# Moving three pieces of preparation in a two-block kernel: a matrix quarter, a square root, and the row of inverse sums

## The chip, the cores and the metric

The kernel runs on one core of one Trainium2 chip. A core has five engines that run side by side, each through its own list of instructions in order: TensorE (PE in the profile, with its weight loads as PEld), VectorE (DVE), ScalarE (ACT), GpSimd (POOL) and SyncE (SP, which here issues nearly all transfers). They meet at semaphores. The metric is the device time of one execution in microseconds. The kernel before takes 1575.92 us, the median of three runs (1575.31 to 1576.35).

## The reference

Two blocks follow each other. The first is attention with a threshold, over 8 batches of 8 heads, 576 rows and 64 columns:

```python
scores = scale * np.matmul(q, k.transpose(0, 1, 3, 2))
thresh = np.max(scores, axis=-1, keepdims=True) - tau
scores = np.where(scores >= thresh, scores, -1000000000.0)
scores = scores - np.max(scores, axis=-1, keepdims=True)
attn = np.exp(scores)
attn = attn / (np.sum(attn, axis=-1, keepdims=True) + 1e-09)
return np.matmul(attn, v).astype(np.float32)
```

The heads are put side by side into x (8, 576, 512). The second block mixes x by a Fourier transform over rows and columns, normalizes each row, and runs two matrices with a relu between them:

```python
u = x + np.real(np.fft.fft(np.fft.fft(x, axis=1), axis=2))
un = (u - mean(u)) / np.sqrt(var(u) + 1e-06)
out = u + np.maximum(un @ w_ch1, 0.0) @ w_ch2
```

w_ch1 is 512x2048 and w_ch2 2048x512, and both arrive as 64-bit floats. All work on the chip is in 32-bit floats.

## The kernel before

**Steps.** Work goes by pairs of heads, four pairs to a batch, five steps to a pair: four steps of 128 rows of both heads, and one that takes the last 64 rows of both. So a batch is 20 steps; steps are counted through: 0 to 19 are the first batch (`step`, L1509), 20 to 39 the second (`second_batch`, L1661), the rest a third loop (L1743). The order of every engine's list is the order in which this Python code emits instructions (a schedule by hand); the only choice left to a planner is `fill`, which emits matmuls of the second block up to a budget counted in matmul columns.

**One step** in the first two batches. `scores` (L451, L457) multiplies into two PSUM tiles. `softmax` (L463) takes the row maximum on VectorE (neg, L472), the exponential on ScalarE (e, L480) with a small threshold instruction (thr, L484), and the comparison and sum on VectorE (e, L488). `inverse` (L394) turns the sums into den (L396, L399) on VectorE. `transposed_weights` (L568) then turns the weights of the step before on TensorE (pe L598 and L601, pw L616), and ScalarE copies them out of PSUM (ends L604 or L608, e_t L618 or L620). In these two batches the division is made late: `spread_inverse` (L512) copies den over 128 columns into rec (L520) on ScalarE, rec is turned along with the weights of that step one step later (L601), and VectorE multiplies by it after the product with v (x, L656). In a pair's fifth step, `spread_inverse` also copies the end of e (L515). From the third batch on, e is divided at once (L560) and rec isn't needed.

**Converting the matrices.** Each 128x512 piece ("chunk") of the two matrices goes through `convert` (L279): a transfer, two bit operations on VectorE (L296, L299), two ScalarE instructions (L304, L307), one VectorE sum (L311), a GpSimd product (L316), and last a sign on ScalarE (L318) with a second GpSimd product (L319). A chunk takes two steps. `softmax` calls its VectorE parts and L316 between the maximum and the exponential (argument `meanwhile`). Its last stage, L318 and L319, is called by the argument `behind`, after the exponentials and before the inverse. The L304 and L307 of the next chunk follow after the weights' copies, and `spread_inverse` is the last thing of a step. The first matrix's first three quarters (12 chunks) are converted in steps 0 to 12; its last quarter and the second matrix in steps 20 to 39, after `PLAN`, which has two chunks at once in steps 25, 30, 32 and 35.

**Centring.** The mean over the rows of the first matrix is taken off it. For each quarter `column_means` (L371, 4 matmuls of 512 columns into pm) is followed by a ScalarE copy (`copy_mean`, L1591) and one step later by `mirrored` (L381, two matmuls into pr) and four `less_mean` (L387, two on VectorE, two on GpSimd). In the first batch they take the place of `busy` (pd, L111), one or two matmuls whose result nobody reads. Quarters 0, 1 and 2 stand in steps 7 and 8, 10 and 12, 14 and 15. The last quarter is centred in steps 29 and 31.

**Mixing of the first batch** in steps 20 to 22: VectorE folds (L698 to L760), six products py (L770) copied by ScalarE (L775), then pa (L787) and the sums u_t (L812, L816) on GpSimd and VectorE. The first product of the hidden layer, ph (L913), reads u_t. Each block of ph has 4 matmuls and a relu, on ScalarE (L918) for even blocks and VectorE (L920) for odd ones. After every third, `Rows.load` turns 128 rows of u (pn, L862), ScalarE copies them out (L867, L868) and VectorE takes their statistics (L873, L874).

**Square root.** `Rows.factors` (L883) takes the square root of the variances (L885) and then one exponential of a constant (L888). For the first group of rows it is called after block 12, in step 36. For all other groups a list, `wanted`, is looked at in the third loop after the division of e.

**PSUM and queues.** The tiles of pe, pw, pv, pm, pr, pn, py, pa and ph share four banks, given out in turn as they come free. SyncE's queue holds the loads of q, k and v, the two small transfers that swap rows of x (L672, L674), and the chunks' loads (L286), in the order of emission.

Of the kernel before, what the change touches and what calls it, by code (L numbers as in the profile page):

```python
# [47 lines left out]
def kernel(  # L48
# [12 lines left out]
    nc = tc.nc  # L61
# [7 lines left out]
    NJ = HID // 128  # L69
# [390 lines left out]
                )  # L460
        steps[i] = (sc, nh)

    def softmax(i, between=None, meanwhile=None, behind=None):  # L463


        t = i % NT
        sc, nh = steps[i]
        neg = sb.tile([128, 2], FP32, tag="neg", bufs=3, name="neg")
        thr = sb.tile([128, 2], FP32, tag="thr", bufs=3, name="thr")
        e = sb.tile([128, 2 * S], FP32, tag="e", name="e")  # L470
        for j in range(nh):
            nc.vector.tensor_reduce(  # L472
                out=neg[:, j : j + 1], in_=sc[j][:, :, 0:HALF], axis=AXIS_XY, op=ALU.max,
                negate=True,
            )
        if meanwhile is not None:
            meanwhile()
        for j in range(nh):
            ej = e[:, S * j : S * (j + 1)].rearrange("p (c n) -> p c n", c=2)
            nc.scalar.activation(  # L480
                out=ej, in_=sc[j][:, :, 0:HALF], func=ACT.Exp, bias=neg[:, j : j + 1], scale=1.0
            )
            if j == 0:
                nc.scalar.activation(  # L484
                    out=thr[:, 0:nh], in_=neg[:, 0:nh], func=ACT.Identity,
                    bias=thr_off[:, :], scale=-1.0,
                )
            nc.vector.scalar_tensor_tensor(  # L488
                out=ej, in0=sc[j][:, :, 0:HALF], scalar=thr[:, j : j + 1], in1=ej,
                op0=ALU.is_ge, op1=ALU.mult, accum_out=den_eps[i % 3][:, j, 0:1],  # L490
            )
            if between is not None and j == 0:
                next(between)
        if behind is not None:
            behind()
        den = inverse(i, nh)
        if between is not None:
            for _ in between:
                pass
        if normalized(i // NT):  # L500
            nc.vector.tensor_scalar(
                out=e[:, 0:S], in0=e[:, 0:S], scalar1=den[:, 0:1], scalar2=None, op0=ALU.mult
            )
            if nh == 2:
                nc.scalar.activation(
                    out=e[:, S : 2 * S], in_=e[:, S : 2 * S], func=ACT.Copy, scale=den[:, 1:2]
                )
            steps[i] = (e, None)
        else:
            steps[i] = (e, den[:, 0:nh])  # L510
# [57 lines left out]
    def transposed_weights(i):  # L568
        for _ in weights_in_parts(i):
            pass  # L570
# [337 lines left out]
    def channels(rows):  # L908
        for j in range(NJ):
            ht = hs[:, BT * j : BT * (j + 1)]  # L910
            ph = ps.tile([128, 512], FP32, tag="mm", bufs=4, name="ph")
            for c in range(ND):
                nc.tensor.matmul(  # L913
                    ph[:, :], w1[c][:, 128 * j : 128 * (j + 1)], u_t[:, c, 0:BT],
                    start=(c == 0), stop=(c == ND - 1),
                )
            if j % 2 == 0:
                nc.scalar.activation(out=ht, in_=ph[:, :], func=ACT.Relu)  # L918
            else:
                nc.vector.tensor_relu(ht, ph[:, :])  # L920
            yield 4 * ND * BT
            if j % 3 == 2 and j // 3 < 4:
                rows.load(j // 3)
                yield ND * 128
            if j == 12:
                rows.factors()
        def both():
            yield from w1_forms()
            ensure(1)
            while not next(forms_w2):  # L930
                yield

        forms = both()
        for t in range(4):
            po = ps.tile([128, DM], FP32, tag="mm", bufs=4, name="po")
            for j in range(NJ):
                nc.tensor.matmul(  # L937
                    po[:, :], hs[:, BT * j + 128 * t : BT * j + 128 * (t + 1)], w2[j],
                    start=(j == 0), stop=(j == NJ - 1),
                )  # L940
                if j % 2 == 1 and j < NJ - 1:
                    next(forms, None)
                    yield 2 * 4 * DM
            rows.add(t, slice(0, DM), po[:, :])
            rows.store(t)
            background()
            yield 2 * 4 * DM
        for _ in forms:
            pass
# [499 lines left out]
    wanted = []  # L1449
# [59 lines left out]
    def step(i):  # L1509

        n, t = divmod(i, NT)
        scores(i)

        def stages(count):
            for _ in range(count if i - 1 in chunks else 0):
                next(chunks[i - 1], None)

        def next_stages():
            if i in chunks:
                next(chunks[i])  # L1520
            stages(2)

        def last_stage():
            stages(1)
            chunks.pop(i - 1, None)

        if t == 1 and n > 0:
            softmax(i, values_in_parts(n - 1, 1), next_stages, last_stage)
            load_v(n + 1)
        elif t == 3:  # L1530
            softmax(i, values_in_parts(n, 0), next_stages, last_stage)
        else:
            softmax(i, None, next_stages, last_stage)
        if t == 1 and n > 0:
            pass
        elif later and later[0][0] <= i:
            later.pop(0)[1](i)
        else:
            busy(2 if i < NCHUNK else 1)
        if t == 3:  # L1540
            prep_pair(n + 1)
        if t == 1:
            prep_ends(n)
        if i > 0:
            transposed_weights(i - 1)
        if t == 2:
            scale_q(n + 1)
        if i in chunks:
            next(chunks[i])
        while after and after[0][0] <= i:  # L1550
            after.pop(0)[1]()
        if i > 0 and i + 3 < NCHUNK:
            chunks[i + 3] = w1_chunk(i + 3)
        if t == 2 and n > 0:
            folds.append(fold_rows(n - 1))
        if folds and next(folds[0], True):
            folds.pop(0)
        spread_inverse(i)
        if i == 5:
            copy_seq()  # L1560
        if i == per_batch - 4:
            fold_halves(0)
        if i >= per_batch - 4:
            next(dim_copies)
# [37 lines left out]
    dim_copies = copy_dim(load_dim())  # L1602
    load_v(1)
    LAST = HID // WC - 1
    for g in range(LAST):
        center(g)
    for i in range(per_batch):
        step(i)
# [12 lines left out]
    chunks = {}  # L1621

    def advance(at):
        for run in chunks.get(at, ()):
            next(run, None)
# [35 lines left out]
    def second_batch(i):  # L1661
# [8 lines left out]
        if first == 0:  # L1670

            transposed_weights(i - 1)
        softmax(
            i, None, lambda: (advance(first), advance(first - 1), advance(first - 1)),
            lambda: advance(first - 1),
        )
        chunks.pop(first - 1, None)
        if first == 0:
            transfers(first)
        fold_more()  # L1680
        if first == 0:
            weighted_values(n - 1, 1)
            scores(i + 1)
            folds.append(fold_rows(n - 1))
            while folds:
                fold_more()
            load_v(n + 1)
            start_batch(0)
            mix(3)
            mix(3)  # L1690
        elif first == 1:
            mix(3)
            transposed_weights(i - 1)
            mix(2)
            advance(first)
        elif first == 2:
            mix(2)
            transposed_weights(i - 1)
            mix(2)
            weighted_values(n, 0)  # L1700
            advance(first)
        else:
            fill()
            transposed_weights(i - 1)
            advance(first)
            fill()
            if first == 9:
                column_means(LAST)
                copy_mean(LAST)
            if first == 11:  # L1710
                mirrored(LAST)
            for at, c, eng in (
                (11, 1, nc.vector), (11, 3, nc.vector), (12, 0, nc.gpsimd), (13, 2, nc.gpsimd)
            ):
                if at == first:
                    less_mean(eng, LAST, c)
            if t == 3:
                prep_pair(n + 1)
            fill()
            if t == 2:  # L1720
                weighted_values(n, 0)
            if t == 0:
                weighted_values(n - 1, 1)
                folds.append(fold_rows(n - 1))
                load_v(n + 1)
# [5 lines left out]
            fold_halves(1)  # L1731
        if first < 3:
            budget += 3 * per_slot
        spread_inverse(i)

    for i in range(per_batch, 2 * per_batch):
        second_batch(i)
# [158 lines left out]
```

## Time and profile before

| | |
|---|---|
| median of three runs | 1575.92 us |
| the profiled execution's own time | 1573.57 us |
| its span, first to last instruction | 1571.8 us |
| TensorE busy | 1528.5 us, 97% |
| VectorE, ScalarE, GpSimd busy | 1061.0, 918.1, 775.6 us |
| mean granted TensorE clock | 0.992 |
| stretch 0 to 300 us, TensorE busy in each 50 us | 45.0, 47.4, 43.6, 46.2, 46.7, 46.5 |
| stretch 300 to 350 us | 49.8 |

The span is 2 us shorter than the execution's time, which has a little at both ends. TensorE is busy nearly everywhere; what it has of idle time lies in the first 300 us, in the two batches that the change touches. A line of the timeline gives the start and the duration in us, the engine, the line of the kernel, the operation, what it writes and reads, how many, and in brackets the idle time before it and what ended it.

### The profile page before, as it was taken

The numbers are of one execution on the slowest core, as the hardware profiler recorded it, in microseconds if no ns is written. First come the engines' busy times: TensorE is split into PE (matmuls) and PEld (weight loads), VectorE is DVE, ScalarE is ACT, GpSimd is POOL, SyncE is SP. The second block draws the span as 40 slices with busy tenths as digits, with TensorE's granted clock in tenths as the row PEclk, the third lists the DMA queues.
The fourth block names the chain that finished last, engine by engine and source line by source line (L and its number), as shares of the span: only waits on it lengthen the run. The fifth ranks groups of instructions, "written<-read, shape, count | busy, mean of one in ns | idle before, by whom it ended". The sixth has DMA issues, their size and how long they took to land.

```text
span 1571.8 us, 26991 instructions
## 1 busy us (share of the span) xinstructions
PE 1528.5 (97%) x9784; PEld 1190.6 (76%) x9784; DVE 1061.0 (67%) x2119; ACT 918.1 (58%) x1921; POOL 775.6 (49%) x962
## 2 busy tenths in 40 slices
PE   8998999999999999999999999999999999999999
PEld 5555455555788778877788778877787878889999
DVE  7876866846869466766578566856577666746546
ACT  6865767544656676656766566666666666232231
POOL 3753555034455642546254724555264625646735
PEclk9999999999999999999999999999999999999999
DMA  7322332646956354634454344635464434646655
GB/s 176 93 42 92 108 86 64 204 148 184 318 161 207 96 165 129 181 107 144 144 177 145 116 139 148 188 99 157 130 188 134 135 121 151 222 141 234 234 201 182
DMA packets 249291, 239.31 MB, mean 152 GB/s; under 512 B 197027, under 2 KB 218533, under 8 KB 229062
## 3 DMA queue, kind: packets, MB, share of 16 engines
q1 hardware_dynamic: 246646, 237.28, 49.3%
q8 instruction: 78, 1.28, 0.3%
q10 hardware_dynamic: 2512, 0.30, 0.1%
q14 instruction: 55, 0.45, 0.1%
HBM read 205.93 MB, written 31.46 MB: 151 GB/s over the span
## 4 chain that ended last, share of the span: by engine, by line
PE 83%; DVE 10%; ACT 4%; DMA 1%; issue 1%; POOL 1%; SPq 0%; DVEq 0%; ACTq 0%
PE ph L1213 24%; PE po L1400 18%; PE pv L647 9%; PE sc L451 9%; PE pw L616 7%; PE po L937 4%; PE ph L913 2%; PE py L770 2%; PE sc L457 2%; DVE neg L472 1%; PE pa L787 1%; PE pe L598 1%; PE pn L862 1%; PE pa L791 1%; PE po L1379 1%
## 5 line engine op out<-in xcount | busy, mean ns | idle before, releaser
L531 DVE TENSOR_REDUCE neg<-sc 128x1 f32<-128x576 f32 x216 | 154.2, 750 | 132.2 <-PE sc L451 118.3
L537 ACT ACTIVATE e<-sc,neg 128x576 f32<-128x576 f32 x216 | 158.5, 734 | 119.4 <-DVE neg L531 119.4
L1400 PE MATMUL po<-w,w_all 128*128 128x128 f32 x1728 | 219.6, 277 | 0.3 <-ACT ends L604 0.3
L1150 DVE TENSOR_TENSOR hs<-ph,hs 128x512 f32<-128x512 f32 (+1 forms) x128 | 105.3, 823 | 161.3 <-PE ph L1213 102.7
L1400 PEld LDWEIGHTS po<-w,w_all 128*128 128x128 f32 x1728 | 205.5, 192 | 9.2 <-issue 6.2
L1159 POOL TENSOR_TENSOR w<-hs 128x512 f32<-128x512 f32 x32 | 42.0, 1316 | 317.5 <-ACT hs L1155 243.6
L551 DVE SCALAR_TENSOR_TENSOR e<-sc,thr,e 128x576 f32<-128x576 f32 x216 | 168.2, 811 | 19.3 <-ACT thr L541 19.0
L1213 PE MATMUL ph<-u_t,w 128*128 128x256 f32 x768 | 180.5, 381 | 0.6 <-DMA w<-f 0.5
L618 ACT COPY e_t<-pw 128x512 f32<-128x512 f32 x256 | 148.6, 594 | 46.2 <-PE pw L616 45.2
L616 PE MATMUL pw<-ident,e 128*128 128x128 f32 x1152 | 171.7, 277 | 3.6 <-ACT ends L604 1.5
L451 PE MATMUL sc<-kT,qT 64*128 64x288 f32 x1024 | 166.9, 428 | 5.9 <-DVE e L488 4.8
L560 ACT ACTIVATE e<-e,den 128x576 f32<-128x576 f32 x216 | 157.5, 775 | 7.7 <-DVE den L399 7.0
L1213 PEld LDWEIGHTS ph<-u_t,w 128*128 128x128 f32 x768 | 141.2, 190 | 23.4 <-issue 4.5
L1213 PE MATMUL ph<-w_all,w 128*128 128x256 f32 x672 | 157.0, 382 | 1.1 <-DVE w_all L1135 1.0
L616 PEld LDWEIGHTS pw<-ident,e 128*128 128x128 f32 x1152 | 137.3, 142 | 19.7 <-issue 5.6
L1213 PEld LDWEIGHTS ph<-w_all,w 128*128 128x128 f32 x672 | 123.4, 190 | 23.9 <-issue 4.9
L1155 ACT ACTIVATE hs<-hs 128x512 f32<-128x512 f32 (+1 forms) x96 | 74.0, 771 | 113.8 <-DVE hs L1150 113.1
L451 PEld LDWEIGHTS sc<-kT,qT 64*128 64x128 f32 x1024 | 95.3, 186 | 57.1 <-issue 26.0
L1265 POOL TENSOR_TENSOR w_all<-w_all 128x128 f32<-128x128 f32 (+2 forms) x160 | 117.0, 748 | 30.3 <-DVE w_all L1420 22.4
L1400 PE MATMUL po<-w,hs 128*128 128x128 f32 x912 | 119.4, 278 | 0.0
L1400 PEld LDWEIGHTS po<-w,hs 128*128 128x128 f32 x912 | 109.6, 192 | 9.4 <-issue 7.2
L812 POOL TENSOR_TENSOR u_t<-x,tmp 128x289 f32<-128x289 f32 (+1 forms) x45 | 33.7, 748 | 127.5 <-DVE tmp L807 127.5
(236 smaller groups left out, 2946.5 us busy)
## 6 DMA issues: line engine op xcount, KB each, us to landing
w<-f SPq DMA_DIRECT2D x150, 1024.0 KB, 5.0
hs<-in_moe_w_ch_dram SPq DMA_DIRECT2D x20, 512.0 KB, 4.7
q_in<-in_q_dram SPq DMA_DIRECT2D x128, 72.0 KB, 4.2
out_dram<-u SPq DMA_DIRECT2D x36, 256.0 KB, 2.4
k_in<-in_k_dram SPq DMA_DIRECT2D x124, 72.0 KB, 2.5
v_in<-in_v_dram SPq DMA_DIRECT2D x64, 128.0 KB, 5.1
f<-w SPq DMA_DIRECT2D x14, 512.0 KB, 3.6
f<-w SPq DMA_DIRECT2D x7, 1024.0 KB, 4.6
```

What stands on the lines that cost most here:

```text
L451: nc.tensor.matmul(sc[j][:, c, 0:HALF], qT[hp, 128 * t : 128 * t + 128], kT[hp, k0 + HALF * c : k0 + HALF * (c + 1)], start=True, stop=True,)
L531: nc.vector.tensor_reduce(out=neg[:, j : j + 1], in_=sc[j][:, :, 0:HALF], axis=AXIS_XY, op=ALU.max, negate=True,)
L537: nc.scalar.activation(out=ej, in_=sc[j][:, :, 0:HALF], func=ACT.Exp, bias=neg[:, j : j + 1], scale=1.0)
L551: nc.vector.scalar_tensor_tensor(out=ej, in0=sc[j][:, :, 0:HALF], scalar=thr[:, j : j + 1], in1=ej, op0=ALU.is_ge, op1=ALU.mult, accum_out ...
L560: nc.scalar.activation(out=e[:, S * j : S * (j + 1)], in_=e[:, S * j : S * (j + 1)], func=ACT.Copy, scale=den[:, j : j + 1],)
L616: nc.tensor.transpose(pw[:, c, :], e[:, c0 : c0 + 128], ident[:, :])
L618: nc.scalar.copy(e_t[:, 4 * j : 4 * j + 4, qs], pw[:, :, :])
L647: nc.tensor.matmul(pv[64 * j : 64 * j + 64, 0:m], vt[:, 2 * c + j, :], e_t[:, 4 * j + c, 0:m] if c < 4 else ends[:, 0, 0:m], start=(c == 0 ...
L1150: nc.vector.tensor_tensor(out=to, in0=bank, in1=to if other is None else other, op=ALU.add)
L1213: nc.tensor.matmul(bank[:, 256 * q : 256 * q + 256].rearrange("p (two n) -> p two n", two=2), left[:, 256 * c + 128 * q : 256 * c + 128 * ...
L1265: return lambda: eng.tensor_tensor(out=to, in0=to, in1=other, op=ALU.add)
L1400: nc.tensor.matmul(to, lefts[m][j][:, s], right_[:, 128 * s : 128 * (s + 1)], start=jn in (0, 4) and s == 0, stop=s == 3, skip_group_check ...
```

## The change

Three things move, and one argument goes.

1. Quarter 2 of the first matrix is centred later: `column_means` and `copy_mean` go from step 14 into step 20, behind the scores of step 21; `mirrored` and the four `less_mean` go from step 15 into step 21, behind the first products over the rows. Steps 14 and 15 get one `busy` matmul each instead.
2. The first group's square root is no longer taken after block 12: after block 15 the group is put on `wanted`, and the third loop takes it up in step 40.
3. `spread_inverse` moves from the end of a step to directly behind the weights' copies, and the chunk's last stage (sign L318 and product L319), which stood in `softmax` ahead of `inverse`, moves behind it. The argument `behind` is dropped.

```diff
@@ softmax
-        if behind is not None:
-            behind()
         den = inverse(i, nh)
@@ channels
-            if j == 12:
-                rows.factors()
+            if j == NJ - 1:
+                wanted.append(rows)
@@ step
-            softmax(i, None, next_stages, last_stage)
+            softmax(i, None, next_stages)
...
         if i > 0:
             transposed_weights(i - 1)
+        spread_inverse(i)
+        last_stage()
         if t == 2:
             scale_q(n + 1)
         if i in chunks:
...
             folds.pop(0)
-        spread_inverse(i)
@@
-    for g in range(LAST):
+    for g in range(LAST - 1):
         center(g)
@@ second_batch
-        softmax(
-            i, None, lambda: (advance(first), advance(first - 1), advance(first - 1)),
-            lambda: advance(first - 1),
-        )
-        chunks.pop(first - 1, None)
+        softmax(i, None, lambda: (advance(first), advance(first - 1), advance(first - 1)))
+
+        def last_stage():
+            spread_inverse(i)
+            advance(first - 1)
+            chunks.pop(first - 1, None)
+
...
             weighted_values(n - 1, 1)
+            last_stage()
             scores(i + 1)
+            column_means(LAST - 1)
+            copy_mean(LAST - 1)
...
         elif first == 1:
             mix(3)
             transposed_weights(i - 1)
+            last_stage()
             mix(2)
+            mirrored(LAST - 1)
+            for c, eng in ((1, nc.vector), (3, nc.vector), (0, nc.gpsimd), (2, nc.gpsimd)):
+                less_mean(eng, LAST - 1, c)
             advance(first)
         elif first == 2:
             mix(2)
             transposed_weights(i - 1)
+            last_stage()
...
         else:
             fill()
             transposed_weights(i - 1)
+            last_stage()
             advance(first)
             fill()
...
-        spread_inverse(i)
```

More of the change, by code (lines that the diff above doesn't have):

```diff
@@ L461, in scores, with softmax @@
         steps[i] = (sc, nh)
-    def softmax(i, between=None, meanwhile=None, behind=None):
+    def softmax(i, between=None, meanwhile=None):
         t = i % NT
@@ L1527, in step @@
         if t == 1 and n > 0:
-            softmax(i, values_in_parts(n - 1, 1), next_stages, last_stage)
+            softmax(i, values_in_parts(n - 1, 1), next_stages)
             load_v(n + 1)
         elif t == 3:
-            softmax(i, values_in_parts(n, 0), next_stages, last_stage)
+            softmax(i, values_in_parts(n, 0), next_stages)
         else:
-            softmax(i, None, next_stages, last_stage)
+            softmax(i, None, next_stages)
         if t == 1 and n > 0:
```

## The prediction

> **What bounds the kernel now.** I read the page first. TensorE is busy 97% of the span, 99% after 300 us, so only what shortens or lengthens its way through the first 300 us counts. Then the waits of TensorE in the second batch (115 to 285 us; us in total, times, longest):
>
> ```profile
> PE py L770 <- DVE f L755: 3.7, 1, 3.7
> PE pe L601 <- ACT rec L520: 3.1, 3, 2.0
> PE sc L457 <- DVE e L488: 2.5, 1, 2.5
> PE ph L913 <- ACT ends L604: 1.6, 1, 1.6
> PE pe L598 <- ACT e L515: 1.1, 1, 1.1
> PE ph L913 <- POOL u_t L816: 0.6, 1, 0.6
> ```
>
> The change aims at four of these: a hole of 3.7 us before the mixing's products, the waits for rec and e, and ends. Stretches of the granted clock show a second price (stretch, busy us, clock, DMA share, GB/s):
>
> ```profile
> 126.00:128.00 2.00, 0.86 (x4) 0.86 1.16 343
> 128.00:134.00 6.00, 5.94 (x27) 0.50 0.26 85
> 134.00:136.00 2.00, 2.00 (x18) 0.94 0.00 0
> 192.00:196.00 4.00, 4.00 (x10) 0.57 0.17 27
> 260.00:264.00 4.00, 3.62 (x12) 0.57 0.41 131
> ```
>
> Each follows an idle TensorE (3.71, 2.46 and 1.95 us) and lasts 3 to 7 us at half speed. ScalarE's timeline of step 35 shows what stands ahead of rec (bracket: idle before, and releaser):
>
> ```profile
> 246.81 0.58 ACT L620 COPY e_t<-pw 128x512 f32<-128x512 f32 x1
> 247.29 0.63 ACT L304 ACTIVATE w_all<-w_all 128x512 f32<-128x512 int32 x1
> ...
> 249.57 0.25 ACT L867 COPY u<-pn 128x129 f32<-128x129 f32 x1
> ...
> 250.18 0.63 ACT L918 ACTIVATE hs<-ph 128x512 f32<-128x512 f32 x1
> 250.99 0.30 ACT L520 COPY rec<-den 128x128 f32<-128x128 f32 x1 [0.18 <-DVE den L399]
> ...
> 257.05 1.28 ACT L885 ACT_TABLE_LOAD   x1
> ```
>
> Everything between e_t and rec ran while den wasn't there yet: even last in its step rec waited 0.18. VectorE's timeline of that step says who else waits for what rec will hold up:
>
> ```profile
> 250.79 0.17 DVE L399 RECIPROCAL den<-den 128x2 f32<-128x2 f32 x1
> 250.88 0.67 DVE L873 BATCH_NORM_STATS2 stats<-u 128x6 f32<-128x512 f32 x1
> ...
> 251.68 0.46 DVE L656 TENSOR_TENSOR x<-pv,ends 128x320 f32<-128x320 f32 x1
> 252.28 1.42 DVE L472 TENSOR_REDUCE neg<-sc 128x1 f32<-128x576 f32 x2
> ```
>
> The statistics stand right behind den and read u, which ScalarE copied at 249.6; a rec ahead of that copy puts it after den, and so the statistics, x and the next maximum. Last, GpSimd's timeline of step 22, since part 1 gives GpSimd work ahead of these sums and part 3 a product among them:
>
> ```profile
> 143.58 1.29 POOL L319 TENSOR_TENSOR w_all<-w_all,hs 128x512 f32<-128x512 f32 x1
> ...
> 148.72 0.86 POOL L816 TENSOR_TENSOR u_t<-x,tmp 1x287 f32<-1x287 f32 x1
> ```
>
> From L319 to the last sum GpSimd has no pause, and TensorE waits for that sum (the 0.6 above).
>
> **What the Trainium skill says.** "TensorE: Matmul & The Clock Gate", section "What's actually happening": the clock halves after an idle window of about 3.4 us, free-running, and recovers after about as long of work. The trace agrees on the recovery (3 to 4 us at 0.57); here 1.95 us idle was enough, while waits of 1.6 us kept 1.00. The same page, section "Architectural detail", calls ScalarE and VectorE strict FIFO: a waiting rec holds all behind it. "ScalarE: Activation LUTs", section "What ACT_TABLE_LOAD costs", gives about 1283 ns a load; the trace has 1.28 twice. "SBUF — State Buffer", section "Who interferes with whom": tensor_scalar can contend with GpSimd for a port pair. Here L299 takes 0.42 alone, but 1.49 at 66.01 and 239.37 beside GpSimd's less_mean.
>
> **Part 1, the quarter.** Step 14 loses pm (4 matmuls, 3.43 us) for one filler (0.98). Scores of step 15 ended at 93.65; their second PSUM tile is free when step 14's e (L488) ends, 90.72, plus 0.6: 91.3, and VectorE is free at 91.2. So at most 2.3 us come off. In step 15 pr (1.8) becomes 0.98 under a VectorE-ScalarE chain of 2.7 (93.67 to 96.43): nothing, and without that cover 0.8. Two less_mean on VectorE (1.27) are gone behind TensorE's own 5.6 us of work: nothing.
> In step 20 pm fills the hole: scores end at 123.4, 3.44 gives 126.9, and py waits for L755 until 127.1: no cost. The clock then stays full; py and its followers (127.1 to 134.2 at half speed) become bound by ScalarE's copies and end the rows' first products 2.8 earlier, at 134.5 for 137.3. Then pr costs 1.8 on the path: scores of step 22 start at 136.2 for 137.4. But GpSimd: its first u_t sums end at 138.2, less_mean adds 2 x 1.25 (140.7), q_ends 0.5 to 1.1, and L316 (1.3) waits for VectorE's L311. Without port contention that is 140.8, with the two tensor_scalar beside less_mean about 1.1 later. Then come the second sums, behind L808; L319 (1.29) now stands before the last two (1.54). Their end, 149.58 before, becomes 149.5 to 150.5. TensorE is at ph by 145.0, does two matmuls to 146.8 and waits 2.7 to 3.7 us for it, where it waited 0.59: the hole goes from step 20 to step 22, and the clock falls (about 1.7). Bounds -0.1 to +2.6; I take +2.6, as both shorter waits in this trace cost the clock.
>
> **Part 2, the square root.** In step 36 two loads, root and exponential (3.06) held rec: 1.95 idle, then pw 1.90 for 1.04 and ph 4.46 for 3.60, so 3.7 us off. In step 40 it follows the divisions (283.73 to 285.2) and ends at 288.2. The next exponential began at 286.71 and now ends, both halves, at 289.7; VectorE takes it up at 290.35. Hidden by 0.6; without that cover 1.5.
>
> **Part 3, rec and the sign.** No instruction is added; sign 0.57, rec 0.2 to 0.3 change places. Off the path: rec's other waits (0.88, 0.28), e's (1.09), ends behind a sign (0.57). But rec now waits for den, with sign, L304, L307, relu, the copies of u and the next exponential queued behind it, and others wait for those:
> - Steps 0 to 12: ScalarE nearly full. den to rec 0.25, sign 0.57, L304 and L307 1.14, scaling of q 0.67 where there is one, mean copy 0.49, exponential 0.85. In steps 7 and 8 L488 starts 0.65 later than 55.81 and releases the PSUM tile (x L656) on which pw waits: +0.6. In step 12 it is 0.4 more late on VectorE's chain to step 15. With part 1's 2.3 this makes **-1.5** at step 15 (bounds -2.3 and -0.5).
> - Steps 24 to 28: e's wait saved gives 0.84 (ph then waits for the relu). In step 25 rec waits from 166.7 to 168.0; sign and four L304/L307 end at 171.1, the copies of u at 171.7 for 170.0. VectorE's statistics wait, then L920 and x: x ends at 173.7 for 172.1. SyncE's queue holds the row swap for x, v's loads and the chunk load that L296 meets at 182.56: all 1.6 later. In step 27 ph waits for the relu behind sign, L304, L307 (181.8 for 180.5). Scores of step 28 end 1.3 later: **+1.3** (bounds 0 and 2).
> - Steps 32 to 36: ends gives 0.6, the copies of u in step 32 take it back (230.1 for 227.5, statistics and maximum 1.0 later). In step 33 relu makes ph start at 240.1 for 238.6. In step 35 rec stands from 247.9 to den at 251.7 (e follows two transfers): copies of u end at 255.5 for 250.2, x 4.5 later, ph waits for x's bank until 256.8 for 253.3, scores of step 37 end 3.9 later. Part 2's 3.7 is in this stretch: block 14 ends at 266.7 for 266.6. The new idle time of 2.1 us costs 0.5 by the clock where it isn't hidden: together **+0.9** (bounds -3.5, if nobody needs the copies of u, and +2.5).
> Sign and L319 later free staging rooms 0.5 to 3 us later; the next load has two steps (10 us) of cover. Without it, a wait of that size in L296.
>
> Sum: -1.5 + 2.6 + 1.3 + 0.9 = **+3.3 us**. Against the profiled execution 1573.57 + 3.3 = 1576.9; that lies 2.35 below the median, so **1579.2** as a median.
>
> **Rivals.**
> *Waits only move* (no clock loss in step 22, no contention): -1.5 - 0.1 + 1.3 + 0.5 = +0.2, 1576.1. For it: the clock's window is free-running. Against: two of two waits from 1.95 to 2.46 dropped it.
> *The waits go and stay gone*, faster: rec is ready when TensorE asks, and the copies of u have slack. -2.3 - 0.1 - 0.84 - 0.9 - 3.7, and ends 0.5: -8.3, 1567.6. It decides where den comes by the end of e_t: true in steps 24, 31 and 37, but in 25, 32 and 35 den is 1.3, 2.4 and 3.8 late.
> *Idle TensorE at half speed* in steps 27, 33 and 35 also: idle 1.3, 1.8 and 2.1; three times 1.7 on top: +8.4, 1584.3. Against: 1.6 kept the clock.
> *The change doesn't do what it says*: no; the changed program's order has rec directly behind e_t, pm behind the scores of step 21, and two matmuls that now name ScalarE in their waits.
>
> **Numbers.** Forecast 0.5, waits only move 0.3, gone 0.12, half speed 0.08. The forecast's own range is 1577.5 to 1583. Within 0.2% (3.15 us, about what this kernel's measurement tells from no change) lies the second case and 0.16 of the forecast's half: same 0.38, slower 0.42 + 0.08 = 0.50, faster 0.12. The range 1573.5 to 1585.5 leaves out the gain and what lies above the half-speed case.
>
> **What would show it.** Right: py at clock 1.0 from 127; ph's third matmul waiting over 2 us for u_t; rec waiting for den in steps 25, 32, 35; a longer idle before ph by relu and before pw by the copies of u; no table load near 255, two near 284. Wrong: scores of step 15 not earlier (ScalarE's loop is longer than I worked out), step 22 without a clock loss, or VectorE's neg in step 36 no later.

## The result, and the profile after

The changed kernel takes 1591.93 us (median of four runs, 1589.23 to 1594.43) against 1575.8 us: 1.0102 times the time before, with a 95% interval of 1.0082 to 1.0122. That is 16 us slower, where 3.3 us were forecast, and it lies above the range. The profiled execution has a span of 1591.8 us. Below, a gain or loss in us is the ratio's distance from 1 times some 1575 us, and every experiment is measured against runs of the kernel before in the same series. The granted clock isn't what is lost: it is 0.992 to 0.995 in the four runs, and 0.990 to 0.997 in forty of the kernel before.

First the waits of TensorE in the second batch, 115 to 300 us, as they stand after the change (us in total, times, longest):

```profile
PE ph L911 <- ACT u_t L318: 6.1, 2, 3.1
PE ph L911 <- POOL u_t L814: 3.6, 1, 3.6
PE sc L457 <- DVE e L488: 2.9, 1, 2.9
...
PE ph L911 <- ACT hs L916: 1.2, 2, 0.9
PE ph L911 <- ACT ends L602: 1.0, 1, 1.0
```

The waits for rec, for the end of e (L515) and the 3.7 us before py, at which the change aimed, are gone; the wait of sc for e (L488) stays, at 2.9 us for 2.5. In their place stand GpSimd's sums (3.6) and one that the prediction doesn't have: two products of ph wait 3 us each for a sign. The granted clock in stretches (stretch, busy us, clock, DMA share, GB/s):

```profile
128.00:134.00 6.00, 5.92 (x25) 1.00 1.02 340
158.00:162.00 4.00, 3.32 (x8) 0.72 0.00 0
252.00:254.00 2.00, 2.00 (x6) 0.50 0.27 44
276.00:282.00 6.00, 4.86 (x24) 1.00 0.06 4
```

The half speed behind the filled hole is gone, as predicted. It is back behind the new waits at 155 and 248 us, but not behind the equally long one at 274 us; the last section says why. Step 35 on ScalarE, to be laid beside the timeline shown before:

```profile
263.28 0.59 ACT L618 COPY e_t<-pw 128x512 f32<-128x512 f32 x1
266.15 0.30 ACT L518 COPY rec<-den 128x128 f32<-128x128 f32 x1 [2.28 <-DVE den L399]
...
269.65 0.27 ACT L866 COPY u<-pn 128x127 f32<-128x127 f32 x1
```

rec now holds ScalarE for 2.28 us in front of everything that before ran in that time. Behind it VectorE's statistics come late, and x and the maximum with them, as worked out:

```profile
265.89 0.17 DVE L399 RECIPROCAL den<-den 128x2 f32<-128x2 f32 x1
269.96 0.69 DVE L871 BATCH_NORM_STATS2 stats<-u 128x6 f32<-128x512 f32 x1 [3.90 <-ACT u L866]
```

But most of the loss comes earlier. The start of a row maximum (neg, L472; L531 in step 40) in some steps, against the same maximum in the kernel before (us later, one profiled execution each; the experiments follow):

| run | 0 | 13 | 16 | 23 | 26 | 30 | 33 | 36 | 40 |
|---|---|---|---|---|---|---|---|---|---|
| the change | 0.9 | 8.6 | 5.6 | 6.3 | 11.7 | 12.8 | 13.9 | 18.9 | 17.4 |
| e1, quarter alone | 0.5 | 1.6 | -1.2 | 0.0 | 0.9 | -0.5 | -0.5 | -0.2 | -1.9 |
| e2, root alone | 0.4 | 1.5 | 1.5 | 1.5 | 1.5 | 1.5 | 1.5 | 1.5 | -2.4 |
| e3, rec and sign | 1.2 | 9.3 | 9.1 | 8.9 | 13.1 | 13.8 | 14.9 | 19.9 | 18.4 |
| e4, rec alone | 0.3 | 1.6 | 1.8 | 1.7 | 2.1 | 2.7 | 3.2 | 6.4 | 3.8 |
| e5, sign alone | 0.3 | 3.9 | 3.7 | 3.6 | 6.8 | 5.4 | 4.8 | 4.8 | 3.1 |
| e6, no product | 0.3 | 1.1 | -1.9 | -1.2 | 2.5 | 4.7 | 5.8 | 10.5 | 9.0 |
| e7, two signs | 1.0 | 8.4 | 5.9 | 6.6 | 10.4 | 9.5 | 10.5 | 14.7 | 11.2 |
| e8, means later | 0.3 | 8.1 | 5.1 | 5.5 | 8.6 | 7.8 | 8.8 | 13.4 | 14.9 |
| e9, quarter and root | 1.1 | 1.9 | -0.5 | 0.7 | -0.2 | -0.2 | -0.2 | 0.0 | -3.9 |
| e11, best | 0.0 | 0.1 | -2.9 | -1.7 | -3.5 | -3.1 | -3.1 | -3.1 | -7.0 |
| e12, three repairs | 0.3 | 4.9 | 1.9 | 2.4 | 4.3 | 5.2 | 5.8 | 9.8 | 7.2 |

Up to step 13 the kernels e1, e2, e9 and e11 are the kernel before, and they stand 0.1 to 1.9 us later there: that much is chance. Beside a later start, it is the granted clock: 0.51 from 16.3 to 19.8 us in e2, from 81.5 to 85 in e1 and from 82.5 to 86 in e9, and 1.00 there in the kernel before. In the change it is 1.00 from 10 to 88 us too, and yet it stands 8.6 us later, in steps for which +0.6 and +0.4 us had been worked out.

What happens in these steps is seen on VectorE and GpSimd. In the kernel before, step 4:

```profile
29.39 1.30 POOL L319 TENSOR_TENSOR w<-w,hs 128x512 f32<-128x512 f32 x1
...
33.16 0.43 DVE L299 TENSOR_SCALAR hs<-hs 128x512 int32<-128x512 int32 x1
```

After the change, the same step; the sign of step 3 comes behind the copies and rec:

```profile
33.20 0.69 ACT L318 ACTIVATE hs<-hs 128x512 f32<-128x512 int32 x1
34.02 1.55 POOL L319 TENSOR_TENSOR w<-w,hs 128x512 f32<-128x512 f32 x1 [3.17 <-issue]
34.33 1.53 DVE L299 TENSOR_SCALAR hs<-hs 128x512 int32<-128x512 int32 x1
```

In the kernel before, GpSimd's product L319 is over (30.69) well before the next bit operations begin. Moved with its sign, it starts as the next maximum ends and runs beside them: L299 takes 1.53 us for 0.43. Among the 24 bit operations (L296, L299) of the first twelve chunks, two took over 0.7 us before, thirteen after the change, twelve in e3; their sum is 12.5 us before and 19.7 after the change, 7.2 us more. Nine of the thirteen run beside L319, the other four beside GpSimd's less_mean and folds. The bit operations stand between the maximum and e (L488), which frees the PSUM tile for the next scores: on the chain of work and waits that ends last, between 10 us and the maximum of step 13, they hold 4.3 us in the kernel before and 14.5 in the change. The Trainium skill ("SBUF — State Buffer", section "Who interferes with whom") says that tensor_scalar can contend with GpSimd for a port pair; the trace agrees, at 0.3 to 1.1 us a meeting.

### The profile page after: what moved, and what is told of

Read it like the earlier page. It is cut to its first block, busy times and chain, and to the rows that moved or that the text cites. A ratio compares the mean times of both kernels' runs of the same rounds, so it can differ in the third digit from the quotient of the medians.

```text
span 1591.8 us, 26998 instructions
## 1 busy us (share of the span) xinstructions
PE 1538.4 (97%) x9788; PEld 1194.1 (75%) x9788; DVE 1071.4 (67%) x2119; ACT 919.8 (58%) x1921; POOL 776.2 (49%) x962
## 4 chain that ended last, share of the span: by engine, by line
PE 79%; DVE 13%; ACT 4%; DMA 2%; issue 1%; POOL 1%; SPq 0%; DVEq 0%; ACTq 0%; POOLq 0%
PE ph L1211 24%; PE po L1398 18%; PE pv L645 9%; PE sc L451 9%; PE pw L614 6%; PE po L935 4%; PE ph L911 2%; PE py L768 2%; PE sc L457 2%; DVE e L488 2%; DVE neg L472 1%; PE pa L785 1%; PE pe L596 1%; PE pa L789 1%; PE po L1377 1%
## 5 line engine op out<-in xcount | busy, mean ns | idle before, releaser
L451 PE MATMUL sc<-kT,qT 64*128 64x288 f32 x1024 | 172.1, 428 | 9.1 <-DVE e L488 7.8
```

What stands on the lines that cost most here:

```text
L451: nc.tensor.matmul(sc[j][:, c, 0:HALF], qT[hp, 128 * t : 128 * t + 128], kT[hp, k0 + HALF * c : k0 + HALF * (c + 1)], start=True, stop=True,)
```

## The experiments

**One part at a time.** e1 is the kernel before with the quarter moved, e2 with the root moved, e3 with rec and the sign moved.

> The kernel before with part 1 alone (quarter 2 centred in steps 20 and 21). Theory C (the change's loss is part 3's: GpSimd's L319 now runs beside VectorE's L296 and L299): part 1 shortens steps 0 to 15 by about 2.3 us and loses 2 to 4 us in step 22, where the third product of ph waits for GpSimd's sums: -1 to +2 us in all. Theory Q (the loss is mainly part 1's, the hole of step 22 and what follows it): +4 us or more.

> The kernel before with part 2 alone (square root in step 40). Both theories: the idle 1.95 us of TensorE near 258 us and the half-speed stretch behind it go: -2.5 to -3.7 us. If the wait of rec only gives way to another wait in step 36, -1 to 0 us.

> The kernel before with part 3 alone (inverse sums behind the weights' copies, sign behind them). Theory C: L296 and L299 of steps 1 to 12 together take 7 us more, the maximum of step 12 starts about 8 us later, and in steps 33 and 36 ph waits 3 us twice for the sign: +15 to +20 us. Theory Q: +2 to +6 us.

Measured: e1 0.9985 (0.9975 to 0.9995), -2.4 us; e2 0.9977 (0.9966 to 0.9987), -3.6 us; e3 1.0109 (1.0093 to 1.0125), +17.2 us. So parts 1 and 2 are gains and part 3 is the whole loss. e1 did slightly better than theory C said: between the maxima of steps 13 and 16 it wins 2.8 us, and in step 22 ph waits only 1.50 us for GpSimd's sums, with the clock at 1.00 behind it. In e3 the 24 bit operations take 19.0 us for 12.5, and ph waits 3.1 and 3.0 us for the sign. The three add up to +11.2, not +16: about 5 us are lost only when they are together, which is just more than the intervals leave open (4.6).

**Part 3 in halves.** e4 moves rec and leaves the sign; e5 moves the sign and leaves rec.

```diff
@@ e4, on the kernel before (step; alike in second_batch)
             transposed_weights(i - 1)
+        spread_inverse(i)
...
-        spread_inverse(i)
@@ e5, on e3 (step; alike in second_batch)
-        spread_inverse(i)
         last_stage()
...
+        spread_inverse(i)
```

> The kernel before with half of part 3: the inverse sums directly behind the weights' copies, the sign left behind the exponentials. Theory C: GpSimd's L319 stays where it was, so steps 0 to 12 lose at most 2 us and ph waits for no sign; only the waits of rec for den in steps 25, 32 and 35 cost, 1 to 4 us: +1 to +6 us. Theory W (ScalarE held up by rec's wait for den is what costs, wherever the sign is): +10 us or more, most of what part 3 costs as a whole.

> The kernel before with the other half of part 3: sign L318 and product L319 behind the weights' copies, the inverse sums left at the end of a step. Theory C (GpSimd's L319 now runs beside VectorE's L296 and L299, and two signs release a room in u_t late): most of part 3's +17 us without any wait of rec ahead of the sign, +8 to +14 us, L296 and L299 of steps 1 to 12 together 5 us or more above the kernel before. Theory W (it takes rec's wait for den to make the sign late): +1 to +4 us.

Measured: e4 1.0018 (1.0007 to 1.0029), +2.8 us; e5 1.003 (1.0018 to 1.0041), +4.7 us. For e4 theory C holds: bit operations 12.4 us, no wait for a sign, and by step 13 no loss beyond chance; it loses 3 us between steps 33 and 36, where den is late in step 35. For e5 theory C missed, and 4.7 lies just above theory W's +1 to +4, whose upper part the interval (2.8 to 6.5) takes in. The contention is there (16.0 us for 12.5), but only half as large, and the waits for a sign are short:

```profile
PE ph L911 <- ACT u_t L318: 1.5, 2, 1.0
```

Neither half carries the loss: 2.8 and 4.7 against 17.2 for both. Theory C was incomplete, and theory W as e4 has it (+10 or more with rec alone) was wrong.

**The product taken away.** e6 is the changed kernel without L319 in the first twelve chunks. Their signs are not multiplied in, all else stays.

```diff
         nc.scalar.activation(out=sign, in_=high, func=ACT.Sign)
-        nc.gpsimd.tensor_tensor(out=dst, in0=dst, in1=sign, op=ALU.mult)
+        if product:
+            nc.gpsimd.tensor_tensor(out=dst, in0=dst, in1=sign, op=ALU.mult)
```

> The changed kernel without GpSimd's product L319 in the first twelve chunks (the signs of these three quarters are computed but never multiplied in; everything else, the place of the sign on ScalarE too, is as in the changed kernel). Theory C: L296 and L299 of steps 1 to 12 fall back to 0.42 us each and the step loop with them: 7 to 9 us less than the changed kernel by step 12, so about +7 to +9 us over the kernel before. Theory W (ScalarE's order makes the steps longer): no gain before step 12, within 2 us of the changed kernel.

Measured: 1.0069 (1.0054 to 1.0084). The two bit operations of the step shown above, with nothing on GpSimd beside them (the lines have other numbers here):

```profile
32.83 0.41 DVE L300 TENSOR_SCALAR w<-hs 128x512 int32<-128x512 int32 x1
33.16 0.41 DVE L303 TENSOR_SCALAR hs<-hs 128x512 int32<-128x512 int32 x1
```

All 24 take 10.5 us, none over 0.7, and the maximum of step 13 stands at +1.1 for +8.6, inside what chance gives, with the change's order on ScalarE kept. So the loss of the first batch is the product's, not ScalarE's. At the end 5 us are won, not quite the 7 to 9 expected: the second batch loses as before.

**The sign's room.** In steps 33 and 36 the chunk's raw words lie in room "u", columns of u_t behind those that ph reads (L355). The two waits stand just there:

```profile
247.38 1.08 ACT L616 COPY e_t<-pw 128x512 f32<-128x512 f32 x2
250.03 0.30 ACT L518 COPY rec<-den 128x128 f32<-128x128 f32 x1 [1.58 <-DVE den L399]
250.24 0.66 ACT L318 ACTIVATE u_t<-u_t 128x512 f32<-128x512 int32 x1
...
250.95 1.13 PE L911 MATMUL ph<-u_t,w 128*128 128x512 f32 x2 [3.06 <-ACT u_t L318]
```

The sign writes into u_t, though not into the columns that ph reads. A product of ph that the program puts behind it waits for it all the same, and it waits for rec, and rec for den. e7 puts the signs of these two steps back.

```diff
+        softmax(i, None, lambda: (advance(first), ...),
+                (lambda: advance(first - 1)) if first in (13, 16) else None)
...
-            advance(first - 1)
+            if first not in (13, 16):
+                advance(first - 1)
```

> The changed kernel with the signs of steps 33 and 36 alone (the two steps that free a room in u_t) back behind the exponentials. If the two waits of ph of 3.1 and 3.0 us are for these signs, both go, with the half-speed stretches behind them: 5 to 8 us less than the changed kernel. If ph waits there for rec or a copy of the weights, the waits stay and the time is within 1 us of the changed kernel.

Measured: 1.0083 (1.0071 to 1.0095), 3 us less than the change where 5 to 8 were expected; the intervals of the two leave 3.7 us open. The waits are for these signs: both are gone from the list, and from step 30 to 40 the profiled execution loses 1.7 us, the change 4.6. But the time isn't all won, since the next late thing of the same queue, the copies of u behind rec, holds pw instead:

```profile
PE pw L616 <- ACT u L868: 2.6, 1, 2.6
```

**GpSimd's less_mean.** e8 is the change with the two GpSimd less_mean of the moved quarter in steps 23 and 24.

```diff
-            for c, eng in ((1, nc.vector), (3, nc.vector), (0, nc.gpsimd), (2, nc.gpsimd)):
+            for c, eng in ((1, nc.vector), (3, nc.vector)):
...
+            if first in (3, 4):
+                less_mean(nc.gpsimd, LAST - 1, 2 * (first - 3))
```

> The changed kernel with GpSimd's two less_mean moved from step 21 to steps 23 and 24. If the 3.6 us wait of ph in step 22 is GpSimd's 2.7 us of less_mean, it falls to about 1 us and the half-speed stretch of 1.7 us goes with it: 3 to 5 us less than the changed kernel. If it is VectorE's late bit operations and second sums that hold GpSimd, 0 to 1.5 us less.

Measured: 1.0076 (1.0063 to 1.0088), 4 us less, just more than the 3.7 that the intervals leave open. The wait in step 22 falls, and the clock in 156 to 162 us is 1.00:

```profile
PE ph L911 <- POOL u_t L814: 1.7, 1, 1.7
```

**The order of the two.** e10 is the change with sign and product ahead of rec.

> The changed kernel with the last stage (sign L318, product L319) and the inverse sums in the other order behind the weights' copies: the sign first, rec second. Rec alone cost 2.9 us and the sign alone 4.7, both together 17. Theory I (they add up to more because the sign, standing behind rec, waits for den too, and with it the next chunk's L304 and L307 and the product): the sign comes 0.5 to 2 us earlier in every step, ph waits for it twice by at most 1 us, and the time is 6 to 11 us less than the changed kernel's, +4 to +10 us over the kernel before. If the order of the two does not matter (ScalarE is simply over-full between the copies and the next exponential): within 2 us of the changed kernel.

Measured: 1.0054 (1.0039 to 1.0069), 7.6 us less than the change, where the intervals leave 3.9 open. Theory I holds by the time; its trace isn't drawn on here, so what the theory says of the waits of ph stays unseen. The halves of part 3 don't add: rec alone waits for den, but the sign has gone ahead of it; the sign alone waits for nothing but the copies; behind rec it waits for den as well, as in the lines of step 33 above.

**Three repairs at once.** e12 has e10's order, e7's two signs and e8's less_mean.

> The changed kernel with three repairs at once: the sign ahead of rec, the signs of steps 33 and 36 behind the exponentials, and GpSimd's two less_mean in steps 23 and 24. Alone they took 0.48, 0.19 and 0.26 per cent off the changed kernel's +1.02. If they are three separate causes and all of the loss but rec's own waits: +0.0 to +0.3 per cent over the kernel before (0 to +5 us). If they overlap (the sign ahead of rec already frees most of the room in u_t): +0.3 to +0.5 per cent (+5 to +8 us).

Measured: 1.0036 (1.0022 to 1.0049), +5.7 us: they overlap. No wait for a sign is left. What remains by step 13 (+4.9, bit operations 16.1 us) is e5's contention, and between steps 33 and 36 it loses 4 us like e4.

**A version that beats both.** e9 is the kernel before with the quarter, the root and the later less_mean; e11 also has rec directly behind the copies, but in steps 24 and 31 alone.

```diff
+            if first in (4, 11):
+                spread_inverse(i)
             advance(first)
...
-        spread_inverse(i)
+        if first not in (4, 11):
+            spread_inverse(i)
```

> The kernel before with parts 1 and 2, without part 3, and with GpSimd's two less_mean of the moved quarter in steps 23 and 24. If the parts add: -2.4 (part 1) and -3.6 (part 2), and 0 to -1.5 us for the wait of ph in step 22: -6 to -7.5 us. If the clock's stretches merely move elsewhere when the waits move: -2 to -4 us.

> The last kernel with the inverse sums directly behind the weights' copies in steps 24 and 31 alone, where den ends 0.3 to 0.4 us before the copies do. If rec ahead costs only where it waits for den: another 0.5 to 2 us less than that kernel. If rec ahead gains nothing even there: within 0.5 us of it.

Measured: e9 0.9976 (0.9963 to 0.9989), -3.8 us: not the sum of the parts, but the second case, in which the clock's stretches move elsewhere. e11 has 0.9955 (0.9942 to 0.9969), -7.1 us, the fastest of all (median 1565.6). The two profiled executions differ by 5.5 us, and of these the trace shows 0.9 as e11's own, between the maxima of steps 23 and 26, where the wait for the end of e (1.1 us) is gone. 1.8 us lie before step 13, where the programs are the same, and 1.7 in the clock in this stretch, first in e9 and then in e11:

```profile
276.00:284.00 8.00, 8.00 (x29) 0.79 0.98 289
```

```profile
276.00:284.00 8.00, 8.00 (x41) 1.00 1.01 337
```

In both, TensorE stands idle for the same 1.56 us ahead of step 40. The mean clock is 0.996 to 0.998 in all five runs of e11 and 0.992 to 0.996 in the seven of e9. Whether that is e11's own doing isn't shown, so more than the 0.9 can't be put down to it.

## Why the prediction was wrong, step by step

- **Direction and the stage of part 3**: slower was right, the size was not. The profiled executions differ by 20.0 us in span. To step 13 the change loses 7.7 us beyond its late start, wins 3.0 by step 16, loses 7.2 to step 30 and 4.6 to step 40; the rest lies in the start (0.9) and behind step 40 (2.6). The terms for these were +1.0, -2.3, +3.9 and +0.9. Two of the sums don't come out of their terms: -2.3, +0.6 and +0.4 give -1.3 at step 15, not -1.5, and the 0.1 and 0.5 worked out for steps 32 to 36 give 0.6, not 0.9. Neither slip bears on the result.
- **The step that failed, first batch**: part 3's "No instruction is added; sign 0.57, rec 0.2 to 0.3 change places", with +0.6 in steps 7 and 8 and +0.4 in step 12. It followed the sign along ScalarE, and not the product that the sign releases on GpSimd. The price was in hand (L299 "takes 0.42 alone, but 1.49" beside GpSimd's less_mean), but was applied only to part 1. Measured, +7.2 us of bit operations on the loop of steps 1 to 12; without the product the loss is gone (e6).
- **The second step that failed**: that the later sign only frees staging rooms late, with "two steps (10 us) of cover". Loads have that cover; ph doesn't, since a room lies in u_t. The prediction mentioned "two matmuls that now name ScalarE in their waits" as proof of the order and gave them no price. Measured, 3.1 and 3.0 us of idle, of which removal returned about 3 us (e7).
- **Part 1** was right in what it fills and in where the hole goes, and too dear. The quarter wins 2.8 in steps 13 to 16 (e1) for 2.3, and the clock is 1.00 from 128 us on. py ends 2.5 us earlier relative to the rest (138.15 less 6.5 of delay, against 134.16), and the rows' first products 1.7 (142.17 less 6.5, against 137.37) for 2.8; so the scores of step 22 start no earlier (143.98 less 6.5), where 1.2 had been counted. The new wait in step 22 is 3.58 for 2.7 to 3.7, with a clock of 0.72. It needs both parts: part 1 alone has 1.50, part 3 alone 2.2. Alone, part 1 was to cost -2.3 + 2.6 = +0.3 and gained 2.4 (e1), with no fall of the clock in step 22. That the clock falls there was luck in part: in e7's execution the same 3.6 us are followed by 1.00.
- **Part 2**: -3.7 was forecast, -3.6 measured alone (e2), and the loads stand behind the divisions at 302.6. There they are hidden, as forecast: the change stands 17.4 us later at the maxima of steps 40, 42 and 50 alike. But parts 2 and 3 each remove the same wait: e3, with the root still in step 36, has no wait for rec there either. The root's gain came once, not on top of rec's.
- **rec waiting for den** in steps 25, 32 and 35, with the copies of u and x behind it, was right in mechanism, and in two of three sizes: 1.46, 2.33 and 2.28 us for 1.3, 2.4 and 3.8. But rec waits in steps that weren't named as well, 2.04 in step 22, 3.72 in step 27 and 1.58 in step 33, and the last of these stands ahead of the sign in u_t. e4 sizes rec's waits at +2.8 us in all. In step 27 ph's wait for the relu is 0.9.
- **The rivals**: "idle TensorE at half speed" has longer idle times near steps 33 and 35 than it named (3.06 and 3.00 for 1.8 and 2.1), but for the sign and not for what it named, and half speed behind the first alone; its 1584.3 is too low by 7.6. "Gone" decides where den comes by the end of the copies: steps 24 and 31 bear this out in e11, by 0.9 us at least.

Not settled: which part of the 7.2 us between steps 16 and 30 is the late sign and which the quarter. In e8 2.7 of it are left, e3 alone has 4.7.

## What to carry to other kernels

When an instruction is moved, move in the prediction everything it releases on other engines as well, and lay each of these beside what now runs at that moment: in the first batch the sign cost next to nothing on ScalarE and 7 us through GpSimd. An instruction that may wait belongs ahead of others only where its input is surely there; two moves that are cheap alone can cost more than twice their sum when one queues behind the other. A wait that a changed program newly names is a price to be worked out, not a remark.

## What the runs showed of the hardware

The granted clock after an idle TensorE is less a matter of the idle time's length than I had taken it to be. In the change 3.06 us of idle ending at 251 us were followed by 0.50, and 3.00 ending at 277 us by 1.00. The falls of the clock show the reason. In the kernel before, the first three begin at 127.43, 192.28 and 260.55 us, which is 19 and 20 times 3.413 us apart. In the change they begin at 159.79, 204.16 and 251.95, 13 and 14 times as much, and each lasts 3.41 us, or now and then twice that. So what counts is how much of one such window TensorE stands idle. The windows around the two waits (stretch, TensorE's busy us, clock, DMA share, GB/s):

```profile
248.48:251.89 3.41, 0.94 (x2) 1.00 0.00 0
251.89:255.31 3.42, 3.42 (x13) 0.51 0.29 46
272.37:275.78 3.41, 1.77 (x5) 1.00 0.00 0
275.78:279.20 3.42, 2.06 (x10) 1.00 0.00 0
```

The first wait lies mostly in one window, the second is split over two. In the thirteen profiled executions drawn on here, from 20 us on, each of the 35 windows in which TensorE was idle for 58% or more was followed by half speed, and none of the 5817 with less than 44%; in between it was 30 of 69. The idle shares come from the matmul records, whose ends are modelled. The 1.56 us ahead of step 40 are such a case in between: 46% of one window in e9, where the clock fell, and 45% in the kernel before, where it didn't.

The Trainium skill ("TensorE: Matmul & The Clock Gate", section "What's actually happening") calls the window free-running, and that fits; but its idle window of 3.4 us is no bound below which nothing happens here, since about half of one was enough. As the windows lie differently in each execution, the same wait costs a fall in one and none in another. A fall costs at most half of its 3.41 us, 1.7 us. In 40 runs of the unchanged kernel, which spread from 1568.87 to 1578.34 us, time and mean clock (0.997 to 0.990) go together, with a correlation of -0.96.
